# A long convolution by FFT before a soft mixture of experts: whole-tile stores, and DRAM layouts to match

## The chip, the cores and the metric

The kernel runs on one core of one Trainium2 chip. The metric is device time in microseconds for one execution; a time is a median of several runs, and one further execution was taken with the hardware profiler.

## The reference, cut to what matters

```python
# x: (8, 5696, 128), h: (5696, 128)          B, S, D
L = 2 * S
y = irfft(rfft(x, n=L, axis=1) * rfft(h, n=L, axis=0)[None], n=L, axis=1)[:, :S, :]
x = y.reshape(B * S, D)                       # 45568 tokens
logits = x @ phi                              # (45568, 32), 8 experts with 4 slots each
d = softmax of logits over the tokens;        slot_input = d.T @ x
slot_out[e] = relu(slot_input[e] @ w1[e]) @ w2[e]
c = softmax of logits over the slots;         out = c @ slot_out
```

Everything is float32.

## The kernel before, in words

The convolution is a transform of N = 5760 = 90 x 64 points with half-sample shifts. N1 = 90 is the length of the first factor, N2 = 64 that of the second, HALF = 32, CH = 4, NJ = 8. Group g = 0 is the filter h, and g = 1 to 8 are the batches of x.

**Stage A** (`stage_a`, words `low` and `high` in the order of work) does the 90-point half. `load_x` brings rows of x, two slots of CH columns n with their mirrored columns, `fold` (GpSimd) makes sum and difference of the two (o = 0, 1), and TensorE multiplies by the table `s1`. The 64 lower of the 90 frequencies come from `low`, the 26 upper ones from `high`, which serves two slots at once. One PSUM bank holds four matmul results of 32 partitions each, ACT copies it to the staging tile `fst` (four buffers), for the two parts (real, imaginary) one after the other. Then `fst` is stored to DRAM, `fl[g]` or `fh[g]`. In `fst` the partition runs over (o, frequency k1) for `low`, with even and odd k1 (a = 0, 1) alternating, so the two stores take `st[0::2]` and `st[1::2]`, 64 partitions each, with rows of 1024 bytes.

**Stage B** reads the spectra back transposed. `load_g` (word `loadf`) loads a tile `gt` (three buffers): partitions are the 64 values of the second index for each of a = 0, 1, and a row holds up to four frequencies of 1024 bytes side by side. There are 12 such units in a group, eight from `fl` and four from `fh`, the last of them with one frequency. `stage_b1` (word `forward`) multiplies by `wt` on TensorE and by the filter's spectrum `Hr`, `Hi` on VectorE; `stage_b2` (word `backward`) transforms back with `vt`, and ACT copies the result to `zst`, one tile of four slots. After every second unit two slots are stored: the first 64 frequencies to `zm`, the other 26 to `zr`. The partition of `zst` runs over (a, r, o) with o alternating, and each store takes `sv[o::2]`.

**Stage C** does the 90-point half back. `load_main` and `load_rest` (words `load`, `loadz`, `loadr`) load `zc` from `zm` (1 MB, rows of 8192 bytes) and `zx` from `zr` (0.5 MB, rows of 4096 bytes). There are 32 steps T, four for each batch. They share one pair of tiles until the last steps, when a second pair (`zd`, `zy`) joins. `stage_c1` (word `product`) multiplies with `im` and `ir`, and the rest of the step turns the result, makes logits and both softmaxes and gathers the slot inputs. After the last step come the experts and the output.

All loads and stores of this are issued by SP in the order of the strings given to `run`; stores are collected in `pending` and issued at the next word `flush`. SP issues in that order, so an issue that waits holds back all that follow it. A small part of the start goes through ACT's queue: five tables, and eight fills of rows of `zr` with zeros from the tile `zx`.

The DRAM layouts before, slowest index first: `fl` (a, j, n, (o, k), x), `fh` (a, pair, n, (slot, o, k), x), `zm` (o, k, r, part, d), `zr` (o, part, k, r, d). In each of them the loads see 128 rows at one constant distance:

```python
src = fl[g].rearrange("a j n (o k) x -> (a j n o) (k x)", o=2)                 # load_g, 269
in_=zm[b].rearrange("o k r c d -> (o k) r (c d)")[:, j * n:(j + 1) * n]...     # load_main, 377
```

Of the kernel before, what the change touches and what calls it, by code (L numbers as in the profile page):

```python
# [19 lines left out]
def transform_tables(S, N1, N2, CH, LOW, MAIN):  # L20

    N, R1, HALF, P = N1 * N2, S // N2, N2 // 2, 2 * N2  # L30
    k1 = np.arange(N1)
    alpha = np.pi * (k1 + 0.5) / N1
    m1 = np.arange(R1) - (N1 - 1) / 2
    a1 = np.outer(m1, alpha)
    part = np.stack([np.cos(a1), -np.sin(a1), -np.cos(a1)], 1)
    s1 = np.zeros((P, 3, N2 + HALF))
    for p, r in ((slice(0, P, 2), slice(0, N2)), (slice(P - 4 * (R1 - N2) + 1, P, 4), slice(N2, R1))):
        s1[p, :, 0:LOW] = part[r, :, 0:LOW]
        s1[p, :, N2:N2 + N1 - LOW] = part[r, :, LOW:]
    a0 = np.outer(alpha, np.arange(N1 // 2) + 0.5)  # L40
    part = np.stack([np.cos(a0), -np.sin(a0), -np.cos(a0)], 1)
    NP = N1 // 2
    im = np.zeros((2, MAIN, 2, N2))
    ir = np.zeros((2, 2, HALF, N2))
    for o in range(2):
        for c in range(2):
            im[o, :, c, 0:NP] = part[0:MAIN, o + c]
            ir[o, c, 0:N1 - MAIN, 0:NP] = part[MAIN:, o + c]
    k2 = np.arange(N2)
    omega = np.pi * (k1[:, None] + 2 * N1 * k2[None] + 0.5) / N  # L50
    m2 = np.arange(HALF) - (N2 - 1) / 2
    a2 = m2[None, :, None] * omega[:, None, :]
    w = np.concatenate([np.cos(a2), np.sin(a2)], 1)
    back = np.arange(N2).reshape(2, HALF).T.reshape(-1)
    NU = (NP + 1) // 2
    turn = (N1 - 1) / 2 * alpha[:, None] + (N2 - 1) / 2 * omega
    wq = np.zeros((2, N2, NP, N2))
    vq = np.zeros((2, N2, NU, 2, N2))
    tn = np.zeros((2, N2, 2, (NU + 1) // 2, 2, 2))
    rows = np.arange(N2).reshape(2, HALF // CH, CH)  # L60
    near = rows.transpose(1, 2, 0).reshape(-1)
    far = rows.reshape(2, -1, 2, CH).transpose(1, 3, 2, 0).reshape(-1)
    for a in range(2):
        wq[a] = w[a::2].transpose(1, 0, 2)
        wq[a] = np.concatenate([wq[a][near, 0:LOW // 2], wq[a][far, LOW // 2:]], 1)
        for q in range(NP):
            vq[q % 2, :, q // 2, a] = w[2 * q + a][back].T
            tn[q % 2, :, 0, q // 4, a, q // 2 % 2] = np.cos(turn[2 * q + a]) / N
            tn[q % 2, :, 1, q // 4, a, q // 2 % 2] = np.sin(turn[2 * q + a]) / N
    im, ir, wq, vq, tn = [t.reshape(P, *t.shape[k:]) for t, k in  # L70
                          ((im, 2), (ir, 3), (wq, 2), (vq, 2), (tn, 2))]
    return [np.ascontiguousarray(t, dtype=np.float32) for t in (s1, im, ir, wq, vq, tn)]
# [3 lines left out]
def kernel(  # L76
# [47 lines left out]
        nc.inline_tensor(t, f"tab_{n}").ap()  # L124
        for n, t in zip(("s1", "im", "ir", "w", "v", "turn"),
                        transform_tables(S, N1, N2, CH, LOW, MAIN))]
    fl = [nc.dram_tensor(f"fl_{g}", (2, NJ, CH, 2 * LOW // 2, 2 * D), F32, kind="Internal").ap()
          for g in range(B + 1)]
    fh = [nc.dram_tensor(f"fh_{g}", (2, NJ // 2, CH, 2 * HALF, 2 * D), F32, kind="Internal").ap()
          for g in range(B + 1)]  # L130
    zm = [nc.dram_tensor(f"zm_{b}", (2, MAIN, HALF, 2, D), F32, kind="Internal").ap() for b in range(B)]
    zr = [nc.dram_tensor(f"zr_{b}", (2, 2, HALF, HALF, D), F32, kind="Internal").ap() for b in range(2)]
    cd = nc.dram_tensor("c_t", (P, B * NQ, Q, 2, MH), F32, kind="Internal").ap()

    const = ctx.enter_context(tc.tile_pool(name="const", bufs=1))
# [93 lines left out]
    def stage_a(c, high):  # L229

        g, j = divmod(c, NJ)
        st = apool.tile([P, CH, 2, D], F32, name="fst", tag="fst", bufs=4)
        if high:
            groups = [(c_, o, HALF, slice(HP, HP + HALF)) for c_ in (c - 1, c) for o in range(2)]
        else:
            groups = [(c, o, HALF, slice(r, r + HALF)) for o in range(2) for r in (0, HALF)]
        for q in range(2):
            p = bank()
            for i, (c_, o, m, cols) in enumerate(groups):
                nc.tensor.matmul(p[i * m:(i + 1) * m, :], s1[:, q + o, cols], columns(c_, o),  # L240
                                 start=True, stop=True)
            nc.scalar.activation(st[:, :, q, :],  # L242
                                 p[:, :].rearrange("p (n d) -> p n d", d=D), AF.Copy)
        for a in range(2):
            dst = fh[g][a, j // 2] if high else fl[g][a, j]
            pending.append(partial(
                nc.sync.dma_start, out=dst.rearrange("n r x -> r n x"),
                in_=st[a::2, :, :, :].rearrange("r n c d -> r n (c d)")))
        if high:
            for c_ in (c - 1, c):  # L250
                del folded[c_]
# [10 lines left out]
    def load_g(u):  # L262
        if u >= (B + 1) * NW:
            return
        g, w, us = parts(u)
        n = sum(k for _, k in us)
        t_ = bpool.tile([P, 4, 2, D], F32, name="gt", tag="gt", bufs=3)
        if 8 * w < LOW:
            src = fl[g].rearrange("a j n (o k) x -> (a j n o) (k x)", o=2)
        else:  # L270
            src = fh[g].rearrange("a j n (o k) x -> (a j n o) (k x)", o=4)
        k0 = 4 * w % (LOW // 2) * 2 * D
        nc.sync.dma_start(
            out=t_[:, 0:n, :, :].rearrange("p q c d -> p (q c d)"), in_=src[:, k0:k0 + n * 2 * D])
        gs[u] = t_

    def stage_b1(u):
# [38 lines left out]
    def stage_b2(u):  # L316
        g, w, us = parts(u)
        if g == 0:
            return
        m = len(us)  # L320
        y_ = prods.pop(u)
        bz = bps.tile([P, 2, 2, 2 * D], F32, name="bz", tag=("bt", "bz")[u % 2])
        for o, (i, n) in enumerate(us):
            for q in range(n):
                r = slice(q * HP, (q + 1) * HP)
                for a in range(2):
                    nc.tensor.matmul(bz[a * HP:(a + 1) * HP, q, o, :], vt[r, i, a, :],  # L327
                                     y_[r, a * m + o, :, :].rearrange("p c d -> p (c d)"),
                                     start=True, stop=True)
        n = us[0][1]  # L330
        e_ = w % 4
        nc.scalar.activation(zst[:, e_, 0:m, 0:n, :].rearrange("p o q x -> p q o x"),  # L332
                             bz[:, 0:n, 0:m, :], AF.Copy)
        if w % 2 == 0:
            return
        k = 4 * e_ + m * n
        sv = zst[:, :, :, :, :].rearrange("p u o q x -> p (u o q) x")
        q0 = 4 * e_ - 4
        k0 = 8 * (w - 1)
        for o in range(2):  # L340
            if k0 < MAIN:
                pending.append(partial(
                    nc.sync.dma_start,
                    out=zm[g - 1][o, k0:k0 + 16].rearrange("(q a) r c d -> (a r) q (c d)", a=2),
                    in_=sv[o::2, q0:k, :]))
                continue
            for c in range(2):
                pending.append(partial(
                    nc.sync.dma_start,
                    out=zr[g % 2][o, c, k0 - MAIN:k0 - MAIN + 2 * (k - q0)].rearrange("(q a) r d -> (a r) q d", a=2),  # L350
                    in_=sv[o::2, q0:k, c * D:(c + 1) * D]))

    zs, ys, Ls, ds = {}, {}, {}, {}
    ybufs = [ypool.tile([P, Q * CH, D + 1], F32, name=f"y{i}") for i in range(2)]
# [12 lines left out]
    def load_main(T):  # L367
        if T >= NT:
            return
        b, j = divmod(T, NQ)  # L370
        t_ = zring.pop(0)
        zring.append(t_)
        zs[T] = t_
        n = 2 * CH
        nc.sync.dma_start(
            out=t_[0][:, :, :, :, :].rearrange("p h n c d -> p (h n c d)"),
            in_=zm[b].rearrange("o k r c d -> (o k) r (c d)")[:, j * n:(j + 1) * n].rearrange(
                "p r x -> p (r x)"))

    def load_rest(T):  # L380
        if T >= NT:
# [3 lines left out]
        n = 2 * CH  # L385
        nc.sync.dma_start(
            out=t_[1][:, :, :, :].rearrange("p h n d -> p (h n d)"),
            in_=zr[(b + 1) % 2].rearrange("o c k r d -> (o c k) r d")[:, j * n:(j + 1) * n].rearrange(
                "p r x -> p (r x)"))

    def load_pair(T):
        load_main(T)
# [222 lines left out]
    nc.scalar.dma_start(out=turn[:, :, :, :, :], in_=t_turn)  # L615
    nc.scalar.dma_start(out=im[:, :, :], in_=t_im)
    nc.scalar.dma_start(out=ir[:, :], in_=t_ir)
    for i in range(8):
        nc.scalar.dma_start(
            out=zr[i // 4][i // 2 % 2, i % 2, N1 - MAIN:].rearrange("k (j r) d -> (k j) (r d)", r=2 * CH),  # L620
            in_=zring[0][1][0:4 * (HALF - N1 + MAIN), :, :, :].rearrange("p h n d -> p (h n d)"))
    held = {}

    def load_w1(e_):
# [303 lines left out]
```

## Time and profile before

| | |
|---|---|
| median of 3 runs | 815.35 us (813.96 to 817.2) |
| profiled execution | 815.48 us, span 813.7 us |
| TensorE busy | 717.6 us, mean granted clock 0.949 |
| VectorE, ACT, GpSimd busy | 629.5, 429.3, 411.5 us |
| DMA | 167661 packets, 282.51 MB, mean 347 GB/s |
| HBM | 148.54 MB read, 132.53 MB written |

The span runs from the first to the last instruction of the profiled execution; the execution's own time has 1.8 us more around it. Busy times are sums over instructions. The share of the DMA queues in the page is the time that their packets took, against 16 DMA engines over the whole span.

### The profile page before, as it was taken

The page shows a single profiled execution, that of the slowest core. Times are in us where ns is not written, and L with a number is a line of the kernel's source. Part 1 is how long each engine was busy: PE and PEld are TensorE (multiplying, and loading weights), DVE is VectorE, ACT ScalarE, POOL GpSimd, SP SyncE. Part 2 cuts the span into 40 slices and gives each one's busy share as a digit, 9 for nine tenths or more (in the row PEclk, how much of TensorE's full clock was granted, in tenths as well). Part 3 has the DMA queues.
Part 4 walks back from the last instruction along what each step waited for, and adds up shares of the span by engine and source line. Part 5 has one row for each costly group of instructions (what it writes and reads, how often), then busy time and mean ns, then how long its engine had stood idle before and what let it go on. Part 6 is the DMA issues. An engine that isn't in the chain of part 4 may idle for free.

```text
span 813.7 us, 22006 instructions
## 1 busy us (share of the span) xinstructions
PE 717.6 (88%) x8884; PEld 367.0 (45%) x8884; DVE 629.5 (77%) x895; ACT 429.3 (53%) x868; POOL 411.5 (51%) x368
## 2 busy tenths in 40 slices
PE   5767888869999999999999999999998887888893
PEld 1322233324544444444444455554444443356882
DVE  1029987638988998798999899988998997795642
ACT  2323345326666665566666666665664545474532
POOL 5655434224566666466656666655533443587000
PEclk9989999879999999999999999999999999999755
DMA  8999999999999999999999999999999898873998
GB/s 293 359 329 384 328 393 386 323 348 344 367 355 364 395 372 328 369 355 382 353 387 381 384 349 390 379 352 366 341 321 343 301 354 288 318 267 106 378 401 353
DMA packets 167661, 282.51 MB, mean 347 GB/s; under 512 B 11305, under 2 KB 130729, under 8 KB 162345
## 3 DMA queue, kind: packets, MB, share of 16 engines
q1 hardware_dynamic: 166552, 280.02, 96.6%
q8 instruction: 70, 1.15, 0.5%
q10 hardware_dynamic: 1008, 1.10, 0.4%
q14 instruction: 31, 0.25, 0.1%
HBM read 148.54 MB, written 132.53 MB: 345 GB/s over the span
## 4 chain that ended last, share of the span: by engine, by line
PE 55%; DMA 18%; DVE 15%; ACT 4%; POOL 2%; issue 2%; SPq 1%; ACTq 0%; DVEq 0%; POOLq 0%
PE bank L240 17%; PE bt L286 8%; PE bz L327 7%; PE bank L413 6%; DMA out_dram<-o 5%; PE bank L418 4%; DMA zx<-zr 4%; DVE yf L305 4%; DVE bt L305 4%; PE bank L441 3%; DMA xc<-in_h_dram 3%; PE bank L450 2%; DVE yf L312 2%; PE bank L540 2%; PE bank L564 2%
## 5 line engine op out<-in xcount | busy, mean ns | idle before, releaser
L240 PE MATMUL bank<-x,s 128*32 128x512 f32 x1728 | 209.1, 607 | 14.1 <-POOL x L216 8.3
L216 POOL TENSOR_TENSOR x<-xc 128x512 f32<-128x512 f32 x144 | 179.2, 1278 | 81.4 <-PE bank L240 55.5
L242 ACT ACTIVATE fst<-bank 128x512 f32<-128x512 f32 x216 | 125.8, 595 | 87.1 <-PE bank L240 50.7
L286 PE MATMUL bt<-gt,wt 64*64 64x256 f32 x1620 | 117.1, 398 | 27.4 <-DMA gt<-fl 9.4
L332 ACT ACTIVATE zst<-bz 128x1024 f32<-128x1024 f32 x96 | 93.0, 968 | 82.8 <-PE bz L327 72.5
L431 POOL TENSOR_TENSOR y<-y,op 128x512 f32<-128x512 f32 x64 | 78.4, 1225 | 112.8 <-DVE op L405 110.3
L305 DVE TENSOR_TENSOR yf<-bt,Hi 128x1024 f32<-128x1024 f32 x96 | 112.5, 1172 | 17.9 <-PE bt L286 17.8
L312 DVE TENSOR_TENSOR yf<-bt,yf 128x512 f32<-128x512 f32 x192 | 119.3, 663 | 3.3
L240 PEld LDWEIGHTS bank<-x,s 128*32 128x32 f32 x1728 | 56.1, 111 | 130.4 <-issue 90.8
L305 DVE TENSOR_TENSOR bt<-bt,Hr 128x1024 f32<-128x1024 f32 x96 | 113.0, 1177 | 0.0
L327 PE MATMUL bz<-yf,vt 64*64 64x256 f32 x1440 | 101.4, 390 | 4.8 <-DVE yf L312 4.4
L286 PEld LDWEIGHTS bt<-gt,wt 64*64 64x64 f32 x1620 | 54.7, 135 | 89.0 <-issue 28.8
L527 POOL TENSOR_TENSOR L<-L,rs 128x512 f32<-128x512 f32 x32 | 33.7, 1052 | 108.1 <-DVE rs L522 57.2
L327 PEld LDWEIGHTS bz<-yf,vt 64*64 64x64 f32 x1440 | 55.0, 137 | 41.1 <-DVE yf L312 12.9
L431 POOL TENSOR_TENSOR y<-y,om 128x512 f32<-128x512 f32 x54 | 64.3, 1190 | 2.1
L421 ACT ACTIVATE y<-bank 128x512 f32<-128x512 f32 x32 | 19.1, 597 | 87.4 <-PE bank L418 87.4
L441 PE MATMUL bank<-ident,y 109*128 109x109 f32 x512 | 59.2, 261 | 3.7 <-POOL y L431 1.7
L413 PE MATMUL bank<-zc,im 64*64 64x512 f32 x480 | 60.6, 599 | 0.1
L441 PEld LDWEIGHTS bank<-ident,y 109*128 109x128 f32 x512 | 49.7, 141 | 13.3 <-issue 7.4
L443 ACT ACTIVATE yt<-bank 128x360 f32<-128x360 f32 x128 | 52.6, 476 | 4.1 <-PE bank L441 3.9
L305 DVE TENSOR_TENSOR yf<-bt,turn 128x1024 f32<-128x1024 f32 (+1 forms) x12 | 14.1, 1171 | 52.3 <-PE bt L286 52.3
L405 DVE TENSOR_TENSOR y<-bank,y 128x512 f32<-128x512 f32 x32 | 22.1, 691 | 39.7 <-ACT y L421 36.4
(99 smaller groups left out, 881.7 us busy)
## 6 DMA issues: line engine op xcount, KB each, us to landing
fl<-fst SPq DMA_DIRECT2D x144, 256.0 KB, 6.4
gt<-fl SPq DMA_DIRECT2D x72, 512.0 KB, 8.3
zm<-zst SPq DMA_DIRECT2D x64, 512.0 KB, 6.9
zc<-zm SPq DMA_DIRECT2D x30, 1024.0 KB, 8.1
fh<-fst SPq DMA_DIRECT2D x72, 256.0 KB, 7.2
xc<-in_x_dram SPq DMA_DIRECT2D x32, 512.0 KB
out_dram<-o SPq DMA_DIRECT2D x16, 1024.0 KB, 5.2
zx<-zr SPq DMA_DIRECT2D x30, 512.0 KB
```

What stands on the lines that cost most here:

```text
L216: nc.gpsimd.tensor_tensor(out=y_[:, o, :, :], in0=near, in1=far, op=AL.subtract if o else AL.add)
L240: nc.tensor.matmul(p[i * m:(i + 1) * m, :], s1[:, q + o, cols], columns(c_, o), start=True, stop=True)
L242: nc.scalar.activation(st[:, :, q, :], p[:, :].rearrange("p (n d) -> p n d", d=D), AF.Copy)
L286: nc.tensor.matmul(bt[q * HP:(q + 1) * HP, a, o, :], wt[r, 2 * i + q, :], t_[r, 2 * o + q, :, :].rearrange("p c d -> p (c d)"), start=True ...
L305: nc.vector.tensor_tensor(out=p_, in0=pv, in1=h_, op=AL.mult)
L312: nc.vector.tensor_tensor(out=y_[r, 0:k, c, :], in0=pv[:, :, c, :], in1=y_[r, 0:k, c, :], op=op_)
L327: nc.tensor.matmul(bz[a * HP:(a + 1) * HP, q, o, :], vt[r, i, a, :], y_[r, a * m + o, :, :].rearrange("p c d -> p (c d)"), start=True, sto ...
L332: nc.scalar.activation(zst[:, e_, 0:m, 0:n, :].rearrange("p o q x -> p q o x"), bz[:, 0:n, 0:m, :], AF.Copy)
L413: nc.tensor.matmul(ps[o, c][h_ * HP:(h_ + 1) * HP, :], im[r, c, :], zt[r, h_, :, c, :], start=True, stop=False)
L431: eng.tensor_tensor(out=part_, in0=part(v, 0), in1=o_[:, :, :], op=sign)
L441: nc.tensor.transpose(p[:, i * TR:(i + 1) * TR], ys[T][0:TR, k * CH + i, 0:D], ident[0:TR, 0:TR])
L443: nc.scalar.activation(yt[:, k * CH:(k + 1) * CH, :, :], of_tokens(p), AF.Copy)
```

## The change: whole-tile stores

Each pair of stores of `fst` to `fl` or `fh`, and of `zst` to `zm` or `zr`, becomes one store from all 128 partitions. So that this is possible, the columns of the table `s1` are put in the order (a, k) and the row order `back` of `vt` is dropped; `wq` loses the row order `near`. Partitions of the staging tiles then run over (a, o, k) or, for `high`, (slot of the pair, o, a, k), and over (a, o, r). The DRAM layouts follow: `fl` (n, a, o, k, x), `fh` (pair, n, slot, o, a, k, x), `zm` (k, o, r, part, d), `zr` (part, k, o, r, d). The loads take the same rows, of the same length, into the same partitions' halves, through the new layouts. The fills of `zr` become four of 48 rows.

```diff
-        s1[p, :, 0:LOW] = part[r, :, 0:LOW]
-        s1[p, :, N2:N2 + N1 - LOW] = part[r, :, LOW:]
+        for a in range(2):
+            s1[p, :, a * HALF:a * HALF + LOW // 2] = part[r, :, a:LOW:2]
+            s1[p, :, N2 + a * HALF // 2:N2 + (a * HALF + N1 - LOW) // 2] = part[r, :, LOW + a::2]
...
-        wq[a] = np.concatenate([wq[a][near, 0:LOW // 2], wq[a][far, LOW // 2:]], 1)
+        wq[a][:, LOW // 2:] = wq[a][far, LOW // 2:]
...
-            vq[q % 2, :, q // 2, a] = w[2 * q + a][back].T
+            vq[q % 2, :, q // 2, a] = w[2 * q + a].T
...
-    fl = [nc.dram_tensor(f"fl_{g}", (2, NJ, CH, 2 * LOW // 2, 2 * D), F32, kind="Internal").ap()
+    fl = [nc.dram_tensor(f"fl_{g}", (HALF, 2, 2, LOW // 2, 2 * D), F32, kind="Internal").ap()
...
-    fh = [nc.dram_tensor(f"fh_{g}", (2, NJ // 2, CH, 2 * HALF, 2 * D), F32, kind="Internal").ap()
+    fh = [nc.dram_tensor(f"fh_{g}", (NJ // 2, CH, 2, 2, 2, HALF // 2, 2 * D), F32, kind="Internal").ap()
...
-    zm = [nc.dram_tensor(f"zm_{b}", (2, MAIN, HALF, 2, D), F32, kind="Internal").ap() for b in range(B)]
-    zr = [nc.dram_tensor(f"zr_{b}", (2, 2, HALF, HALF, D), F32, kind="Internal").ap() for b in range(2)]
+    zm = [nc.dram_tensor(f"zm_{b}", (MAIN, 2, HALF, 2, D), F32, kind="Internal").ap() for b in range(B)]
+    zr = [nc.dram_tensor(f"zr_{b}", (2, HALF, 2, HALF, D), F32, kind="Internal").ap() for b in range(2)]
...
-            groups = [(c, o, HALF, slice(r, r + HALF)) for o in range(2) for r in (0, HALF)]
+            groups = [(c, o, HALF, slice(r, r + HALF)) for r in (0, HALF) for o in range(2)]
...
-        for a in range(2):
-            dst = fh[g][a, j // 2] if high else fl[g][a, j]
-            pending.append(partial(
-                nc.sync.dma_start, out=dst.rearrange("n r x -> r n x"),
-                in_=st[a::2, :, :, :].rearrange("r n c d -> r n (c d)")))
+        if high:
+            dst = fh[g][j // 2].rearrange("n c o a k x -> (c o a k) n x")
+        else:
+            dst = fl[g][CH * j:CH * (j + 1)].rearrange("n a o k x -> (a o k) n x")
+        pending.append(partial(
+            nc.sync.dma_start, out=dst, in_=st[:, :, :, :].rearrange("r n c d -> r n (c d)")))
...
-            src = fl[g].rearrange("a j n (o k) x -> (a j n o) (k x)", o=2)
+            src = fl[g].rearrange("n a o k x -> (a o) n (k x)")
...
-            src = fh[g].rearrange("a j n (o k) x -> (a j n o) (k x)", o=4)
+            src = fh[g].rearrange("p n c o a k x -> a (p n c o) (k x)")
...
-            out=t_[:, 0:n, :, :].rearrange("p q c d -> p (q c d)"), in_=src[:, k0:k0 + n * 2 * D])
+            out=t_[:, 0:n, :, :].rearrange("p q c d -> p (q c d)"), in_=src[:, :, k0:k0 + n * 2 * D])
...
-        for o in range(2):
-            if k0 < MAIN:
-                pending.append(partial(
-                    nc.sync.dma_start,
-                    out=zm[g - 1][o, k0:k0 + 16].rearrange("(q a) r c d -> (a r) q (c d)", a=2),
-                    in_=sv[o::2, q0:k, :]))
-                continue
-            for c in range(2):
-                pending.append(partial(
-                    nc.sync.dma_start,
-                    out=zr[g % 2][o, c, k0 - MAIN:k0 - MAIN + 2 * (k - q0)].rearrange("(q a) r d -> (a r) q d", a=2),
-                    in_=sv[o::2, q0:k, c * D:(c + 1) * D]))
+        if k0 < MAIN:
+            pending.append(partial(
+                nc.sync.dma_start,
+                out=zm[g - 1][k0:k0 + 16].rearrange("(q a) o r c d -> (a o r) q (c d)", a=2),
+                in_=sv[:, q0:k, :]))
+            return
+        for c in range(2):
+            pending.append(partial(
+                nc.sync.dma_start,
+                out=zr[g % 2][c, k0 - MAIN:k0 - MAIN + 2 * (k - q0)].rearrange("(q a) o r d -> (a o r) q d", a=2),
+                in_=sv[:, q0:k, c * D:(c + 1) * D]))
...
-            in_=zm[b].rearrange("o k r c d -> (o k) r (c d)")[:, j * n:(j + 1) * n].rearrange(
-                "p r x -> p (r x)"))
+            in_=zm[b][:, :, j * n:(j + 1) * n].rearrange("k o r c d -> o k (r c d)"))
...
-            in_=zr[(b + 1) % 2].rearrange("o c k r d -> (o c k) r d")[:, j * n:(j + 1) * n].rearrange(
-                "p r x -> p (r x)"))
+            in_=zr[(b + 1) % 2][:, :, :, j * n:(j + 1) * n].rearrange("c k o r d -> o (c k) (r d)"))
...
-    for i in range(8):
+    for i in range(4):
         nc.scalar.dma_start(
-            out=zr[i // 4][i // 2 % 2, i % 2, N1 - MAIN:].rearrange("k (j r) d -> (k j) (r d)", r=2 * CH),
-            in_=zring[0][1][0:4 * (HALF - N1 + MAIN), :, :, :].rearrange("p h n d -> p (h n d)"))
+            out=zr[i // 2][i % 2, N1 - MAIN:].rearrange("k o (j r) d -> (k o j) (r d)", r=2 * CH),
+            in_=zring[0][1][0:8 * (HALF - N1 + MAIN), :, :, :].rearrange("p h n d -> p (h n d)"))
```

More of the change, by code (lines that the diff above doesn't have):

```diff
@@ L53, in transform_tables @@
     w = np.concatenate([np.cos(a2), np.sin(a2)], 1)
-    back = np.arange(N2).reshape(2, HALF).T.reshape(-1)
     NU = (NP + 1) // 2
@@ L60, in transform_tables @@
     rows = np.arange(N2).reshape(2, HALF // CH, CH)
-    near = rows.transpose(1, 2, 0).reshape(-1)
     far = rows.reshape(2, -1, 2, CH).transpose(1, 3, 2, 0).reshape(-1)
```

## The prediction

> **What bounds the kernel now.** I read the page first (engines, slices, queues), then the table of windows by stage, then the list of DMA issues. Of the page these lines carry the argument:
>
> ```profile
> span 813.7 us, 22006 instructions
> PE 717.6 (88%) x8884; PEld 367.0 (45%) x8884; DVE 629.5 (77%) x895; ACT 429.3 (53%) x868; POOL 411.5 (51%) x368
> ...
> DMA  8999999999999999999999999999999898873998
> GB/s 293 359 329 384 328 393 386 323 348 344 367 355 364 395 372 328 369 355 382 353 387 381 384 349 390 379 352 366 341 321 343 301 354 288 318 267 106 378 401 353
> ...
> q1 hardware_dynamic: 166552, 280.02, 96.6%
> q8 instruction: 70, 1.15, 0.5%
> q10 hardware_dynamic: 1008, 1.10, 0.4%
> q14 instruction: 31, 0.25, 0.1%
> ```
>
> Two things are full at once. TensorE is at nine tenths or more in most middle slices, and the 16 DMA engines are too: the queue rows add to 97.6% of 16 engines' span, 794 us for each engine on average. The window of one batch (four output steps) says the same; columns are PE, PEld, DVE, ACT and POOL busy, then granted clock, DMA share and GB/s:
>
> ```profile
> 396.00:473.00 77.00, 76.52 (x986) 38.66 (x979) 70.77 (x99) 49.29 (x99) 47.05 (x40) 1.00 1.04 376
> ```
>
> So a batch takes 77 us, 19.25 us for each step, and no engine has slack with which to hide a slower transfer. What each transfer is, with its issues, size and time to landing, is in the DMA list:
>
> ```profile
> fl<-fst SPq DMA_DIRECT2D x144, 256.0 KB, 6.4
> gt<-fl SPq DMA_DIRECT2D x72, 512.0 KB, 8.3
> zm<-zst SPq DMA_DIRECT2D x64, 512.0 KB, 6.9
> zc<-zm SPq DMA_DIRECT2D x30, 1024.0 KB, 8.1
> fh<-fst SPq DMA_DIRECT2D x72, 256.0 KB, 7.2
> ...
> zx<-zr SPq DMA_DIRECT2D x30, 512.0 KB
> gt<-fh SPq DMA_DIRECT2D x27, 512.0 KB, 8.4
> ...
> zr<-zx ACTq DMA_DIRECT2D x8, 96.0 KB
> ```
>
> **The row that decides.** q10 is the ACT queue: 13 issues, namely five tables of 128 rows and the eight fills zr<-zx of 24 rows. Their data are 5 x 128 + 8 x 24 = 832 packets; the row counts 1008. The other 176 are packets of 4 bytes, the completion marks that each engine taking part writes: 5 x 16 + 8 x 12 = 176, where 16 for every transfer would give 208. So a transfer whose slowest dimension counts 24 was spread over 12 engines, the largest divisor of 24 that is at most 16. The SP queue agrees. Among its packets in the trace 10,744 have 4 bytes, for 672 issues: 672 x 16 = 10,752, eight fewer. One issue has an odd shape, the store of line 896 (128 partitions of the tile against 8 batches by 16 rows in DRAM), and in the trace it has eight late completion marks where others have 16. It used 8 engines although its SBUF side has 128 partitions, so the number has to divide the leading counts of both sides.
>
> **Loads: the diff's side effect.** The stores get a leading count of 128 on both sides. The loads lose it, because o now lies on the other side of n, of k or of a, and the DRAM side no longer folds into one dimension. In the changed program's instructions the DRAM side of gt<-fl leads with 4 (then 32 rows), and those of gt<-fh, zc<-zm and zx<-zr lead with 2 (then 64). By what q10 and line 896 show, these loads run on 4, 2, 2 and 2 engines. Rows keep their lengths, so I price them by the trace's packet records: the median is 159 ns for 4096 bytes, 309 for 8192, 46 for 1024. Time per engine taking part:
> - gt<-fl: 72 issues x 32 rows x 159 ns = 366 us on four engines.
> - gt<-fh: 27 x 64 x 159 ns + 9 x 64 x 46 ns = 275 + 26 = 301 us on two.
> - zc and zd: 32 x 64 x 309 ns = 633 us on two.
> - zx and zy: 32 x 64 x 159 ns = 326 us on two.
>
> If the two are always the same two, and among the four, each of them carries 1626 us of loads. Spread over 16 engines the same packets are 3985 us, 249 us for each engine. Everything else stays spread evenly: 794 - 249 = 545 us by the page's shares, or 494 us with all packets at their medians. I take 520 between them, since the busy ring stretched some packets (4096 bytes: mean 179 against 159) and 14 idle engines will stretch fewer.
>
> Which engines serve a smaller transfer no row names. The two bounds are one fixed set, and a set that moves so that all 16 share evenly (794 us of engine time as now, with only latency lost). I take the fixed set: the eight fills, issued one after another, each show the same 12 by shape alone, and nothing in the trace hints at a cursor. That is an argument, not a measurement. [...]
>
> **Stores.** 344 store issues become 172. Each drops 16 marks of 9 ns: 172 x 16 x 9 ns = 25 us of engine time, 1.5 us for each engine. Data packets keep their 1024 and 512 bytes and their number. SP issues 172 fewer at some 0.65 us, 112 us of SP time; that matters only where SP is late, and SP will be waiting for landings. Each pair already waited for the same ACT evacuation, so no wait is added there. The fills go from eight of 24 rows to four of 48 (16 engines): nothing on the path.
>
> **Edits at nothing.** Tables are constants of the same size. In the low stage the same eight matmuls of 607 ns run with the two inner loops exchanged; the instruction order on PE, DVE, ACT and POOL is otherwise unchanged. Their cover isn't needed: counts and shapes are equal.
>
> **What is late next.** SP issues in order and each engine works its ring in order, so every store and every x load has one sixteenth behind the loads on the first two engines, and completes when these reach it. The wait moves to gt, zc and zx on PE (who waits: DVE at line 305, ACT at 421 and 332, then POOL), and through late stores to fst and zst. None of this adds while the two engines stay busy. They run dry only if SP is blocked with nothing left on them. zc and zx have one buffer for most of the kernel, so the next 30 us of load start after the product has read them; meanwhile up to two or three gt loads (5 or 10 us each) are queued, against a product of 2.9 us on PE plus issue and landing, about 7 us. The stall lies between nothing (always covered) and 32 x 7 = 224 us (never covered); I take 70, nearer to covered, because of those queued gt loads.
>
> **Sum** on the profiled execution's own time, 815.48 us (span 813.7 and 1.8 around it; the median shown, 815.35, is the same within 0.02%): 1626 + 520 - 1.5 + 20 (now idle on the DMA side, 813.7 - 794: start, and the experts before the output) + 70 + 1.8 = 2236, say 2240 us. Low end: 1626 + 494 + 20 - 1.5 + 1.8 = 2140. High end: the page's mean rate instead of packet medians. 282.5 MB over 16 x 794 us is 22.2 GB/s for each engine; the first two would carry 42.3 MB of loads (103.4 MB in all) and 11.2 MB of the rest, 53.5 MB, or 2405 us, with 20, 224 and 1.8: 2650.
>
> **Rivals.**
> - *The set moves.* Loads are confined, but in turn to different engines. Then only latency counts: a step is product, 7 us, then zc at 19.8 us (64 x 309 ns) with zx beside or behind it (10.2): 27 to 37 us in place of 19.25. With 164 us up to the first product and 94 after the last (the first and last matmuls of zc start at 163.5 and 719 us), and 31 steps at the middle, 32: 1250 us. For it: no row names engines. Against: nothing shows turning.
> - *The loads aren't confined (faster).* If the engine number followed the 128 SBUF partitions alone, loads stay on 16 and only the stores' gain is left: 1.5 us of engine time, and at each of eight batch ends two issues of 0.65 us less between the last zr stores and the zx load, which stands in the chain of waits (4% "DMA zx<-zr"): about 10 us with the start's fl stores, so 804 us; PE at 76.5 of 77 us in the batch window caps it from there. It decides as soon as the four loads complete with 16 marks. Against it stand the 176 marks and line 896. The change would then do what its words say and no more.
> - *Confined, and the pairs get in each other's way.* The store of line 896 took about 2.0 us for 16 packets of 2048 bytes, by the distance of its marks from those of the store before, against 16 x 84 ns = 1.3: 1.5 times. If the four-engine loads suffered that, 183 us more: 2420. Against: the loads of x and the stores from half the partitions keep the shortest packet times.
>
> **How the numbers follow.** Forecast 0.81; crowded pairs 0.07; moving set 0.07; not confined 0.05, of that 0.03 faster and 0.02 within 0.5% (about what a measurement of this kernel can tell from no change). So slower 0.95, same 0.02, faster 0.03. The range runs from just under the low end, 2130, to 2600, which takes in the crowded pairs and most of the high end (the last 50 us need every stall and the mean rate together) and leaves out the other two rivals, 0.12, with a little of the forecast.
>
> **What would show it.** In the profile of the changed kernel: q1 keeps its 280 MB with fewer packets (344 stores less 172 remove 2752 marks; the loads' marks fall to 4 or 2); q10's marks are 5 x 16 + 4 x 16 = 144 beside 832 data. The DMA digits fall to 3 or 4 in the middle, GB/s to about 125, with PE near 3. zc takes 20 us or more to land, zx 10 or more, gt<-fl over 5. PE's longest waits name gt, zc and zx. The batch window grows from 77 to about 240 us: per batch the first two engines have 8 x 5.1 + 3 x 10.2 + 2.9 + 4 x 19.8 + 4 x 10.2 = 194 us of loads and some 45 of the rest. Wrong, if DMA stays at nine tenths (moving set, or no confinement), if the landing of zc stays near 8 us, or if the batch is far above 240 us with the two engines not continuously fed (stalls mis-sized).

## The result

The changed kernel takes 2183.24 us (median of 6 runs, 2180.38 to 2183.79), against 814.65 us for the kernel before in the same comparison: 2.680 times as long (95% interval 2.673 to 2.686). The forecast was 2240 with 2130 to 2600. The profiled execution took 2180.42 us, of which the span is 2178.6.

**The page of the changed kernel**, the same lines as before:

```profile
span 2178.6 us, 21764 instructions
...
PE 943.6 (43%) x8884; PEld 440.9 (20%) x8884; DVE 626.8 (29%) x895; ACT 433.4 (20%) x868; POOL 408.7 (19%) x368
...
DMA  8545443234232343334233333234322313322249
GB/s 295 175 128 194 151 145 108 95 123 150 104 118 101 123 131 101 111 123 137 104 118 125 115 121 104 105 125 132 110 101 106 122 72 114 105 88 82 91 155 376
...
q1 hardware_dynamic: 161536, 280.00, 37.3%
...
q10 hardware_dynamic: 976, 1.10, 0.2%
```

The digits of DMA fell from 9 to 2, 3 and 4 for the most part soon after the first `loadf`, and return to 9 only in the last slice, where the output is stored. The bytes are the same (280.00 MB on q1). So a DMA engine is idle nearly two thirds of the time on average, in a kernel that waits for DMA. The instruction counts of PE, DVE, ACT and POOL are the same as before; PE's busy time rose from 717.6 to 943.6 us while its granted clock fell from 0.949 to 0.671 in the mean.

**Completion marks.** q10 lost 32 marks by the four fills of 48 rows: 976 = 832 + 5 x 16 + 4 x 16. q1 lost 5016 packets: 172 stores x 16 = 2752, and the marks of the loads, 72 x 12 + (36 + 64) x 14 = 2264, together exactly 5016. The trace has 5728 packets of 4 bytes on q1, which is 72 x 4 + 36 x 2 + 64 x 2 for the confined loads, 8 for the odd store and 327 x 16 for all others. So the numbers of engines, read as marks for each issue, are 4 and 2, as forecast.

**Windows, one batch each** (columns as before):

```profile
586.00:827.00 241.00, 98.80 (x952) 44.95 (x952) 69.31 (x96) 47.85 (x97) 46.76 (x40) 0.67 0.34 118
827.00:1069.00 242.00, 102.40 (x952) 46.76 (x952) 68.00 (x96) 48.38 (x97) 46.81 (x40) 0.68 0.35 118
```

A batch takes 241 to 242 us; the forecast's account for it was 194 of loads and some 45 of the rest on the two confined engines.

**Waits** (engine and line, for whom; total us, times, longest):

```profile
ACT y L418 <- PE bank L415: 941.5, 32, 38.7
...
PE bank L410 <- DMA zc<-zm: 499.5, 30, 24.0
...
PEld bank L415 <- DMA zx<-zr: 282.8, 30, 18.4
...
ACT fst L241 <- DMA fh<-fst: 148.4, 20, 12.5
...
PE bt L286 <- DMA gt<-fl: 132.7, 30, 14.8
```

The product's matmuls wait 30 times for zc and then 30 times for zx, which lies behind it: SP issued a zc at 887.05 us and a zx at 888.36, and with two packets in flight the records have the 8192-byte rows of the one from 892.4 to 913.0 us and the 4096-byte rows of the other from 912.1. ACT, then VectorE and GpSimd wait for that product. The fourth line is a store that is late: fst is not free until its store has landed, and a part of the store lies behind the loads. Of the 1024 packets of two stores issued at 863.96 (fh) and 872.65 us (fl), 896, or 14 of 16 shares, start from 873.1 to 876.1 us; then 4096-byte rows run alone, two in flight, up to 884.1, the other rows of 1024 bytes start only there, and ACT waits for fst until 888.16. With the loads on 16 engines (experiment 1) the whole wait is 13.4 us in place of 148.4.

**The chain of waits, in order of time** (start, us, what), four batch ends of it:

```profile
585.88 31.53 DMA zx<-zr
...
827.04 36.92 DMA zx<-zr
...
1068.95 36.46 DMA zx<-zr
...
1310.64 37.23 DMA zx<-zr
```

241.2, 241.9 and 241.7 us lie between them. Of the whole chain DMA has 75% (zx<-zr 20%, fh<-fst 17%, gt<-fh 15%) and PE 10%. Times to landing, which the prediction named as a sign, do not stand in this kernel's list of issues; the chain's longest pieces of zc and zx take 26 to 38 us, where the kernel before had landings of 8 us for zc.

### The profile page after: what moved, and what is told of

Read it like the earlier page. It is cut to its first block, busy times and chain, and to the rows that moved or that the text cites. A ratio compares the mean times of both kernels' runs of the same rounds, so it can differ in the third digit from the quotient of the medians.

```text
span 2178.6 us, 21764 instructions
## 1 busy us (share of the span) xinstructions
PE 943.6 (43%) x8884; PEld 440.9 (20%) x8884; DVE 626.8 (29%) x895; ACT 433.4 (20%) x868; POOL 408.7 (19%) x368
## 3 DMA queue, kind: packets, MB, share of 16 engines
q1 hardware_dynamic: 161536, 280.00, 37.3%
## 4 chain that ended last, share of the span: by engine, by line
DMA 75%; PE 10%; SPq 9%; DVE 2%; issue 1%; ACT 1%; POOL 1%; another core or an unknown queue 1%; DVEq 0%; ACTq 0%; POOLq 0%
DMA zx<-zr 20%; DMA fh<-fst 17%; DMA gt<-fh 15%; DMA zc<-zm 6%; DMA gt<-fl 5%; DMA fl<-fst 5%; SPq L273 4%; PE bt L286 3%; SPq L223 2%; DMA cl<-c_t 2%; SPq L198 2%; PE bank L239 2%; DMA out_dram<-o 2%; DMA zr<-zst 1%; PE bz L327 1%
## 5 line engine op out<-in xcount | busy, mean ns | idle before, releaser
L410 PE MATMUL bank<-zc,im 64*64 64x512 f32 x480 | 112.0, 1058 | 499.5 <-DMA zc<-zm 499.5
L286 PE MATMUL bt<-gt,wt 64*64 64x256 f32 x1620 | 171.6, 550 | 265.7 <-DMA gt<-fl 132.7
L239 PE MATMUL bank<-x,s 128*32 128x512 f32 x1728 | 228.4, 660 | 12.4 <-POOL x L215 8.4
L241 ACT ACTIVATE fst<-bank 128x512 f32<-128x512 f32 x216 | 124.8, 595 | 328.6 <-DMA fh<-fst 148.4
L415 PE MATMUL bank<-zx,ir 26*64 26x512 f32 x480 | 60.4, 1082 | 233.6 <-DMA zx<-zr 233.6
L286 PEld LDWEIGHTS bt<-gt,wt 64*64 64x64 f32 x1620 | 73.3, 183 | 367.5 <-issue 184.2
L410 PEld LDWEIGHTS bank<-zc,im 64*64 64x64 f32 x480 | 33.3, 214 | 551.4 <-issue 445.4
L327 PE MATMUL bz<-yf,vt 64*64 64x256 f32 x1440 | 137.1, 496 | 1.3 <-DVE yf L312 1.3
L506 POOL TENSOR_TENSOR L<-L,rm 128x512 f32<-128x512 f32 x32 | 33.5, 1047 | 346.0 <-DVE rm L505 344.0
L327 PEld LDWEIGHTS bz<-yf,vt 64*64 64x64 f32 x1440 | 74.0, 181 | 54.8 <-issue 32.5
L505 DVE TENSOR_REDUCE rm<-L 128x16 f32<-128x512 f32 x32 | 21.9, 683 | 219.1 <-ACT L L482 219.1
```

The costliest lines, as they stand in the source:

```text
L241: nc.scalar.activation(st[:, :, q, :], p[:, :].rearrange("p (n d) -> p n d", d=D), AF.Copy)
L286: nc.tensor.matmul(bt[q * HP:(q + 1) * HP, a, o, :], wt[r, 2 * i + q, :], t_[r, 2 * o + q, :, :].rearrange("p c d -> p (c d)"), start=True ...
L410: nc.tensor.matmul(ps[o, c][h_ * HP:(h_ + 1) * HP, :], im[r, c, :], zt[r, h_, :, c, :], start=True, stop=False)
```

## The experiments

**1. Only the loads, undone.** In the changed kernel, each load in two halves of 64 partitions, so that its DRAM side leads with 32 or 64 rows:

```diff
-            src = fl[g].rearrange("n a o k x -> (a o) n (k x)")
+            src = fl[g].rearrange("n a o k x -> a n o (k x)")
...
-        nc.sync.dma_start(
-            out=t_[:, 0:n, :, :]..., in_=src[:, :, k0:k0 + n * 2 * D])
+        for a in range(2):
+            nc.sync.dma_start(
+                out=t_[a * HP:(a + 1) * HP, 0:n, :, :]..., in_=src[a, ..., k0:k0 + n * 2 * D])
...   # zc from zm[b][:, o, ...], zx from zr[..][:, :, o, ...], o = 0, 1
```

> The changed kernel with each of its loads gt, zc and zx issued as two, one for each half of 64 partitions, so that every load leads with 32 or 64 rows on both sides; whole-tile stores, DRAM layouts, rows and row lengths as in the changed kernel (the row order of wt for the lower frequencies goes with it). SP issues are 672, as many as before the change. Theory (the loss is the number of engines of the loads, the same lowest engines each time): every load is back on 16 engines, engine time is 794 us for each again, so 805 to 825 us, TensorE at 9 tenths. Rival (the new layouts, with rows 32 or 128 KB apart, are slow to read, or whole-tile stores slow to write): most of the loss stays, over 1100 us. Rival (latency of the loads alone, on engines that change): as the theory here.

Measured: 929.94 us (926.76 to 931.37), 1.141 times the time before (1.136 to 1.147). So 1253 of the 1369 us come back with the loads on 16 engines, but 115 do not, and neither theory had that. Lines of its page, and a window:

```profile
DMA  8999998999999999999999999999999999994898
...
q1 hardware_dynamic: 166552, 280.02, 99.5%
```

```profile
340.00:430.00 90.00, 82.90 (x952) 39.21 (x948) 66.79 (x93) 45.78 (x91) 46.07 (x40) 0.95 1.05 306
```

The packets are exactly those of the kernel before, 166552, and the engines are busy all the time, yet move 306 GB/s in place of the 376 of the batch window before (the share adds up the times of the packets, so it can pass 1). So packets got slower: by the trace's records those of 8192 bytes took 548 ns at the median in place of 309, those of 4096 bytes 208 in place of 159, those of 1024 bytes (the whole-tile stores) 46 as before. In the means that is 4960 x (505 - 338) + 28992 x (221 - 179) ns = 2.05 ms of engine time, 128 us for each of 16, 52 in the 8192-byte packets and 76 in those of 4096 bytes: enough for the 115. Either the new layout in DRAM is slower to read, or 64 adjacent partitions are slower to write.

**2. The stores as halves too.**

```diff
-            nc.sync.dma_start, out=dst, in_=st[:, :, :, :]...
+        for r in (slice(0, HP), slice(HP, P)):
+            ... nc.sync.dma_start, out=dst[r], in_=st[r, :, :, :]...      # zst likewise
```

> As the kernel with halved loads, and in addition each store as two of 64 adjacent partitions, in the same layouts: 844 SP issues. It prices the whole-tile stores by themselves. Theory: 172 more stores cost 172 x 16 marks of 9 ns, 1.5 us for each DMA engine, and 112 us of SP issue time that is hidden as long as SP waits for buffers anyway (its longest waits before the change add to some 300 us): 0 to 10 us slower than with whole stores. Rival (what the words of the change say matters: SP's issues are on the path): 10 to 60 us slower.

Measured: 987.47 us (983.62 to 995.67), ratio 1.214 (1.207 to 1.221): 57 us slower than with whole stores, as the rival had it. But the packets got slower again: those of 1024 bytes now take 75 ns or more in their slowest tenth (46 in experiment 1), their mean went from 47.5 to 51.3 ns, and all packets together take 44 us more for each engine, 21 of them in the 1024-byte ones. So SP's issues need not be the reason; the next run separates the two.

**3. Two stores from alternate partitions**, in the new layout, the rest as in experiment 1:

```diff
-        for r in (slice(0, HP), slice(HP, P)):
+        for r in (slice(0, P, 2), slice(1, P, 2)):
```

> The kernel with halved loads and whole-tile stores, with each store made two again, from alternate partitions as before the change, in the new layouts: 844 SP issues. Beside the kernel with whole-tile stores it prices what the words of the change are about, with the target of the loads unchanged. Theory (adjacent halves made the two-store kernel slow, and the number of stores hardly matters): 1.5 us of marks for each engine, 0 to 10 us slower than whole stores, 930 to 940 us. Rival (172 more issues on SP are what cost 57 us there): 975 to 990 us.

Measured: 941.1 us (933.9 to 948.81), ratio 1.152 (1.145 to 1.158). With the same 844 issues as experiment 2 it is 46 us faster, so the choice of adjacent halves cost that much, and not the number of issues. Against whole-tile stores (929.94) it is 11 us slower by the medians, just outside the 0 to 10 expected, and 8 us by the ratios, whose intervals overlap. What the words of the change promise, 172 fewer stores, is therefore worth some 8 to 11 us here, not clear of noise, and in a kernel whose loads are halves; no run prices it with the loads of the kernel before.

**4 and 5. Halves of one load, in the old layout.** The kernel before with zc alone in two transfers, once 0 to 63 and 64 to 127, once even and odd partitions:

```diff
-            out=t_[0][:, :, :, :, :]..., in_=zm[b].rearrange("o k r c d -> (o k) r (c d)")[:, ...]
+        for p_ in (slice(0, 64), slice(64, P)):          # 5: (slice(0, P, 2), slice(1, P, 2))
+            out=t_[0][p_, :, :, :, :]..., in_=zm[b].rearrange("o k r c d -> (o k) r (c d)")[p_, ...]
```

> The kernel before the change with one edit: zc (and zd) is loaded as two transfers, partitions 0 to 63 and 64 to 127, from the old layout; 16 engines for each. It asks what is left in the kernel with halved loads, whose 8192-byte packets took 548 ns at the median in place of 309. Theory (64 adjacent partitions are a slow target for 16 engines, wherever the rows lie in DRAM): 8192-byte packets again near 550 ns; 32 x 8 x 0.24 = 61 us for each engine, 860 to 885 us. Rival (the new layouts, with larger distances between rows, are slow): 309 ns and 812 to 825 us.

> As the one with halves of adjacent partitions, but the two transfers of zc take alternate partitions, 0, 2, 4 and 1, 3, 5: same rows, same number of issues, same engines. Theory (adjacent partitions): 8192-byte packets stay at 309 ns, 812 to 822 us. Rival (any split of a load costs this, by more issues or shorter shares): near the one with adjacent halves.

Measured: adjacent halves 863.61 us (859.71 to 866.91), ratio 1.060 (1.053 to 1.068); alternate ones 815.87 us (813.69 to 825.32), ratio 1.006 (1.002 to 1.009). The 8192-byte packets took 565 ns at the median and 309. From the list of DMA issues, first of adjacent, then of alternate halves (queue: packets, MB, share of 16 engines; issues: KB each, us to landing):

```profile
q1 hardware_dynamic: 167064, 280.02, 98.6%
...
zc<-zm SPq DMA_DIRECT2D x60, 512.0 KB, 9.7
```

```profile
q1 hardware_dynamic: 167064, 280.02, 96.4%
...
zc<-zm SPq DMA_DIRECT2D x60, 512.0 KB, 7.8
```

Same packets, issues and rows in DRAM; only which partitions, each with its row, go together differs, and it makes 48 us. So adjacency is the cause for zc, and the new layout isn't needed to explain the slow 8192-byte packets of experiment 1. For its 4096-byte packets (gt and zx), 76 of the 128 us, the same cause is likely but not shown: no run splits these loads in the old layout, or over alternate partitions in the new one. Against the layout stands that in the changed kernel, with the same layouts, the medians are 160 and 312 ns, though there few engines read at once. So the packets of 8192 bytes took 1.8 times as long on adjacent halves (565 against 309 ns), and no longer on alternate ones (309). Why adjacency does this, no run shows.

**6 and 7. One kind of load undone at a time**, by the edits of experiment 1: zc and zx in halves, then gt in halves.

> The changed kernel with only zc and zx loaded as two halves (64 leading rows, 16 engines); gt stays on 4 and 2. Theory (the same lowest engines for all confined loads, times add): first two engines have 667 us of gt, 120 of z spread evenly, 520 of the rest, 1307, and some 25 idle: 1310 to 1360 us. Rival (engines change, only latency counts): with the 30 us loads of the single buffer gone a step is bound by gt loads that have three buffers, 815 to 950 us. Rival (confined loads of different shape sit on different engines, so the largest alone counts): about 1190, as zc and zx then never mattered for gt's engines.

> The changed kernel with only gt loaded as two halves (16 engines); zc and zx stay on 2. Theory (same lowest engines, times add): 959 us of zc and zx, 129 of gt spread evenly, 520 of the rest, 1608, and some 25 idle: 1610 to 1660 us. Rival (engines change, only latency counts): 27 to 37 us for each of 32 steps, 1100 to 1400 us.

Measured, in two runs each: 1429.73 us (1428.36 to 1431.1) and 1715.64 us (1714.9 to 1716.37). Both lie above the range of the first theory and far from the rivals, and slow packets, as in experiment 1, account for most of the excess. With zc and zx in halves the mean 8192-byte packet took 594 ns (347 in the changed kernel) and the 4096-byte one 205 (188): 107 us for each engine by the sum used in experiment 1, and 1307 + 25 + 107 = 1439. With gt in halves the 4096-byte packets took 219: 55 us, and 1608 + 25 + 55 = 1688 against 1716. The waits, first with zc and zx in halves, then with gt:

```profile
PE bt L286 <- DMA gt<-fl: 139.6, 32, 14.0
...
PE bank L412 <- DMA zc<-zm: 55.4, 12, 9.6
```

```profile
PE bank L413 <- DMA zc<-zm: 449.4, 30, 17.9
...
PE bt L289 <- DMA gt<-fl: 25.9, 16, 7.3
```

In each kernel the load that is still confined is the one waited for, and the time falls by 754 and 468 us, about the share that the load that was undone had on these engines, less what it takes spread out and what its slow packets add (959 - 120 - 107 = 732 and 667 - 129 - 55 = 483). That the shares add (1439 us by the sum and 1430 measured, 1688 and 1716) means that four-engine and two-engine loads meet on the same engines.

**8 to 10. The number of engines by the row count alone.** The kernel before, old layouts and loads, with zc cut into 124 + 4, 122 + 6 and 112 + 16 rows (the edit of experiment 4 with another border):

> The kernel before the change with zc loaded as 124 and 4 rows from the old layout; by the rule of common divisors both run on 4 engines, 31 + 1 rows each. Theory (always the same lowest engines): 32 x 32 x 309 ns = 316 us in place of 79 on four engines, 794 - 79 + 316 = 1031 and some 20 idle: 1040 to 1070 us. Rival (engines change from one transfer to the next): the load takes 10 us where it took 8, 815 to 870 us. Rival (the number of engines doesn't come from the row count): 812 to 825 us.

> The same with 122 and 6 rows: 2 engines with 61 rows each, then 6 engines with one row. Theory (same lowest engines): 32 x 62 x 309 ns = 613 us in place of 79, 794 - 79 + 613 = 1328 and some 20 idle: 1335 to 1370 us. Rival (engines change): a load of 19 us and a product of 7 in each of 32 steps, 950 to 1100 us. Rival (the row count doesn't matter): 812 to 825 us.

> The kernel before the change with zc loaded as 112 and 16 rows: 16 engines for both, 7 and 1 rows each; as many issues as with 124 and 4 or 122 and 6. Theory: no engine gets more than before; 812 to 825 us, up to 845 if 16 adjacent partitions are a slow target too. Rival (a second issue for each step is what costs in the cuts): as slow as these.

Measured, in two runs each: 1143.12 us, 1388.65 us and 854.44 us. The same bytes in the same two issues for each step cost 331, 576 and 40 us over the kernel before, by no more than where the border lies. Windows in the middle with 124 + 4 and with 122 + 6 rows, and the queue of the latter:

```profile
340.00:440.00 100.00, 68.45 (x760) 32.45 (x752) 58.82 (x84) 38.64 (x78) 41.12 (x35) 0.84 0.80 236
```

```profile
340.00:440.00 100.00, 57.05 (x664) 28.34 (x660) 50.56 (x71) 35.44 (x71) 35.23 (x30) 0.80 0.58 182
```

```profile
q1 hardware_dynamic: 166296, 280.02, 61.8%
```

Against 167064 packets with 64 + 64 rows this lacks 768 marks, 32 x 24: 2 + 6 in place of 16 + 16 for each step, as the common divisors read from the kernel before have it (4 + 4 with 124 gives the same sum). The number of packets in flight at once, which needs no marks, agrees: from 300 to 900 us it is below two for 0.1 us and exactly two for 207 us with 122 + 6 rows, and below four for 2.6 us and exactly four for 109 us with 124 + 4. The engine share falls to 0.80 and 0.58 while the kernel gets slower, which is what confinement to a fixed set looks like; if the set moved, these would have been 815 to 870 and 950 to 1100 us. The times lie above the ranges, 73 us over 1070 and 19 over 1370, and the packets got slower again: with 124 rows the 8192-byte ones took 446 ns in the mean (338 before), 4960 x 108 ns over four engines or 134 us if all of it is theirs; with 122 rows 368, or 73 us over two. The 4096-byte packets slowed too (means of 215 and 209 ns against 179); the records name no engine, so how much of either fell on the confined ones stays open. 112 + 16 rows came out at 854 where 845 was the most expected; its 8192-byte packets took 473 ns at the median. Of these 4960 packets only 512 belong to the transfers of 16 rows, so those of 112 rows, which reach into both halves, are slow as well. Why 7 partitions for each engine are slower to write than 8 was not taken apart.

## Why the prediction was right

**The decisive reading held**: that a transfer's number of engines comes from the leading counts of both its sides, read from 176 marks on q10 and from one odd store. The marks of the changed kernel confirm it to the packet, and experiments 8 and 9 show it with the layout untouched.

**The fixed set**, which the prediction only argued, is shown by additivity (6 and 7) and by the cuts (8 and 9), though each came out 19 to 73 us above its range. Which engines they are stays unnamed, and that they are the lowest, as the expectations say, no run shows; that it is a fixed set is what the time needs.

**The sum.** Counted from the packet records, two or more packets are in flight for 2149 of the 2178.6 us, and for 1197 of the 1200 us from 600 to 1800; for 634 of these exactly two. If these are the two confined engines, as the experiments say, they work for 2149 us against the forecast's 1626 + 520 - 1.5 = 2144.5. Loads priced at median packets (159 and 309 ns) were the right end: in the changed kernel the medians are 160 and 312. That the sum is met within 5 us is in part luck: the 520 for the rest was a choice between 494 (redone by the median of each packet size, 489) and 545, and the count does not part the loads from the rest.

**The term that was off is the stall.** It was put at 70 us between 0 and 224. What is left of the span is 29 us, and by the same count the kernel before has 28, at its start and while the experts run (where the forecast had 20); so the stall is about nothing. 2149.4 + 29.2 + 1.8 = 2180.4, the profiled time. The reason given for a small stall, two or three queued gt loads behind each product, fits this, and would have given nothing if followed to its end; which queued work covered the gaps, gt loads or late stores, no run separates.

**The stores** did what was forecast of them in the changed kernel: they land late behind the loads (148 us of ACT's waits for fst). They do stand in the chain of waits (fh<-fst 17%), but add nothing while the two engines are busy. Taken by themselves they are worth some 8 to 11 us (3 against 1), near the 10 us of the rival on the faster side, but not for its reasons, 1.5 us of marks and earlier issues at the batch ends. In the traces each engine's packets take 10.6 us less with whole stores; 1.6 of these are marks, and 7.9 are packets of 4096 and 8192 bytes, mostly loads, that took less long.

**The rivals.** No confinement and a moving set are refuted. Crowded pairs on the four-engine loads did not show in the time: 4096-byte packets kept a median of 160 ns, though the first three gt loads were crowded (310 ns in the mean over all 4096-byte packets from 49 to 61 us). The prediction's reason against crowding, that stores from half the partitions keep the shortest packet times, was true only of alternate partitions, which is what the kernel before uses.

No run beat the kernel before. Its two transfers from alternate partitions are the cheaper of the two ways of halving (0.6% where zc is split so, 6.0% for adjacent halves). Whether there is a layout in which both the store and the load of one tensor are single transfers on 16 engines stays open: as the kernel is written, the stores need a, o and the row side by side, and the loads need the column or frequency between them.

## What to carry to other kernels

When a layout is changed to suit one side of a round trip through DRAM, write down the leading count of both sides of every transfer that touches it, the untouched loads included, and count completion marks in the profile: marks over issues gave the number of engines here (12 for 24 rows, 16 for 48, 4 and 2 for the changed loads). The cost of a transfer was then its rows over that number, at the time of one packet (159 ns for 4096 bytes, 309 for 8192), added up for the busiest engine and not for the mean: 2144.5 us by the forecast, 2149 counted. The sign was a DMA share of 37.3% beside 499.5 us of waits for zc. If a transfer must be split, try alternate partitions before adjacent halves: here they cost 0.6% where the halves cost 6.0%. Measure any other border; 112 + 16 rows cost 40 us.

## What the runs showed of the hardware that was not expected

Sixteen engines that wrote 64 adjacent partitions took 548 to 565 ns for an 8192-byte row in place of 309 (medians of experiments 1 and 4), and the 34 MB of zc took the kernel 48 to 51 us longer (experiment 4 against 5 and against the kernel before); reading from adjacent halves slowed 1024-byte rows too (mean 51.3 ns, against 47.8 from alternate partitions and 47.5 from all 128). Alternate partitions cost little of either: 309 ns at the median, 0.6% of the time.

SP's issue itself got long in the kernel with confined loads. From SP's timeline, a short issue of the kernel before and two long ones of the changed one (start, us, then the issue):

```profile
418.04 0.32 SPq L273 DMA_DIRECT2D gt<-fh  x1
```

```profile
829.71 17.90 SPq L273 DMA_DIRECT2D gt<-fl  x1
...
891.01 18.46 SPq L273 DMA_DIRECT2D gt<-fh  x1
```

All 72 issues of gt<-fl, before and after (shortest, median and longest in ns, then first and last start in us):

```profile
L273 SPq DMA_DIRECT2D gt<-fl x72: 319/432/1676, 47.9 to 636.3; - x72
```

```profile
L273 SPq DMA_DIRECT2D gt<-fl x72: 508/3594/21025, 48.1 to 1816.7; - x72
```

So the median issue went from 0.4 to 3.6 us and the longest from 1.7 to 21, and SP started nothing else in that time, whichever engines it would use: behind the issue of 17.90 us at 829.71 the next, of a load of x, starts at 847.71. What holds the issue no record names; that the confined engines are behind is a guess. In this kernel it cost no more, because two or more packets were in flight meanwhile (1197 of 1200 us).
